# Decode attention on one core: V29 loaded in front of K31, five projections moved behind V29's products, the last projection's weights in three parts

## The chip, the cores and the metric

The kernel runs on one core of one Trainium2 chip. A core has a matrix engine (PE, TensorE), a vector engine (DVE, VectorE), a scalar engine (ACT), GpSimd (POOL) and a queue processor (SP) that here issues nearly all transfers; sixteen DMA engines carry them. The metric is the device time of one execution in microseconds. The kernel before takes 526.45 us (median of 3 runs, 526.36 to 526.49).

## What is computed

One decode step: layer norm of x (4 rows of 640), attention of 32 heads over the last W = 2048 positions of a cache of 8192, a gated feed-forward block, and the sum of both with x. All arrays are bf16.

```python
W = min(4096, max(256, Sk // 4))                      # 2048
q = (xn @ wq).reshape(B, 1, 32, 192).transpose(0, 2, 1, 3)
k = k_cache[:, :, Sk - W:, :]                         # 4 x 32 x 2048 x 192
v = v_cache[:, :, Sk - W:, :]
scores = einsum("bhqd,bhkd->bhqk", q, k) * 192 ** -0.5
o = einsum("bhqk,bhkd->bhqd", softmax(scores), v)
A = o.transpose(0, 2, 1, 3).reshape(B, 1, 32 * 192) @ wo
h = silu(xn @ w1) * (xn @ w3)
out = x + A + h @ w2
```

The K and V windows are 3 MB for each head and kind, 64 such tiles in all; wo is 6144 x 640.

## The kernel before

**Tiles.** A K or V tile holds one head for all 4 batch rows: partition p belongs to batch p // 32, and holds 64 positions of 192 numbers. There are two K buffers (kt) and two V buffers (vt), used in turn by even and odd heads. "K31" is the K tile of head 31, the last one, and so on.

**One head.** VectorE multiplies the K tile by the query in two halves (`mult`, line 271). PE adds the products up over groups of 32 numbers by products with the identity (`adder`, lines 419 and 370), once for each half; VectorE reduces the rest to 64 scores per partition (`reduce_half`, line 277) and takes the maximum over them (`chain_lmax`, 282). PE transposes that column (`tr`, 428), VectorE takes the maximum per batch row (`chain_gmax`, 286), ScalarE scales it (348), PE broadcasts it back over the partitions (`bc`, 432), ScalarE copies it (350) and takes the exponential (352). VectorE spreads the result into z (`chain_z`, 291); PE multiplies z with the V tile in 32 products (`pv`, 445), ScalarE copies the result (355), and PE sums the partial rows (`osum`, 453). For each pair of heads PE makes the softmax sums (`tot`, 437), and VectorE normalizes (`norm_rec`, `norm_og`, 295 and 300); for every fourth head it transposes into oT (303).

**Projections.** `proj(hg)` multiplies the heads of group hg (four heads) with their 768 rows of wo: 6 rows per partition, two products for each, so 12 products of 128x4 by 128x320 (line 382), added into the accumulator acc, in which x and the feed-forward block are already. wo 0 to 4 lie in the buffers wts, loaded during the heads 4 to 8; wo 5, 6 and 7 go into the first K buffer, free once head 30's tile has been multiplied.

**PE's order.** PE runs a hand-written order. A loop takes the heads up to 29 through their adders and up to 28 through their products with V. The end is written out (from line 488): adder 0 of head 30, tr, osum and bc of the heads before, adder 1, tot, proj(0), the products of V29, then the same for head 31 with the products of V30; proj(1), tr of head 31, proj(2), bc, osum of head 30, proj(3), proj(4), tot, the products of V31 in two halves, osum of head 31, and proj(5) to proj(7).

**SP's order.** SP issues transfers in order, and waits in front of each until its buffer is free: `load_k(h)` (line 160) for `s_red` of head h - 2 (its first reduce), `load_v(h)` (168) for `s_pv` of head h - 2 (its products). In the loop of line 181 K(h+2) is followed by V(h+1), up to V28. After the loop come V29, V30 and the two halves of V31, then wo 5, 6 and 7 (lines 197 to 200). So the last tiles come in the order K30, K31, V29, V30, V31. wo 7 comes as five rows and one row, each with a semaphore of its own; PE waits for the first in front of ten products and for the second in front of the last two.

Of the kernel before, what the change touches and what calls it, by code (L numbers as in the profile page):

```python
# [16 lines left out]
def kernel(  # L17
# [15 lines left out]
    B, Sq, D = A_x.shape  # L33
    _, H, Sk, Dh = A_k_cache.shape
# [16 lines left out]
    RPP = QW // P  # L51
# [68 lines left out]
    def sem(name):  # L120
        return ctx.enter_context(nc.semaphore(name))

    first = sem("s_first")
    (s_x, s_wq0, s_wq1, s_wq2, s_w1, s_w3, s_w2, s_k0, s_k1, s_v31, s_wom, s_wo5, s_wo6, s_wo7a, s_wo7b,
     s_gp, s_dv, s_ac, s_pp, s_ps, s_red, s_tr, s_gmax, s_bc, s_negm, s_exp, s_pv, s_sum, s_rec, s_og, s_oT,
     s_tot, s_acc, s_fin, s_done) = [sem(n) for n in (
        "s_x", "s_wq0", "s_wq1", "s_wq2", "s_w1", "s_w3", "s_w2", "s_k0", "s_k1", "s_v31", "s_wom", "s_wo5",
        "s_wo6", "s_wo7a", "s_wo7b", "s_gp", "s_dv", "s_ac", "s_pp", "s_ps", "s_red", "s_tr", "s_gmax", "s_bc",
        "s_negm", "s_exp", "s_pv", "s_sum", "s_rec", "s_og", "s_oT", "s_tot", "s_acc", "s_fin", "s_done")]
    last = sem("s_last")  # L130
    s_pr, s_lmax, s_gneg, s_z, s_v0, s_v1, s_osb, s_out = [sem(n) for n in (
# [4 lines left out]
    def take(e, s, n=1):  # L136
        e.wait_ge(s, n).then_inc(s, -n)  # L137

    def flat(t):
        return (t if isinstance(t, bass.AP) else t[:]).rearrange("p a b -> p (a b)")  # L140
# [5 lines left out]
    def wo_of(hg):  # L146
        t = wts[hg // 2][:, :] if hg < 5 else wo_end
        i = hg % 2 if hg < 5 else hg - 5
        return t[:, i * RPP * D:(i + 1) * RPP * D]

    def wo_src(hg):
        return A_wo[hg * QW:(hg + 1) * QW, :].rearrange("(p i) n -> p (i n)", i=RPP)


    sp = nc.sync

    def load_k(h):
        if h >= 2:
            sp.wait_ge(s_red, 2 * (h - 2) + 1)
        sp.dma_start(out=flat(kt[h % 2]), in_=k_win[:, h].rearrange("b (p j) d -> p b (j d)", p=PB)).then_inc(s_k[h % 2], 16)  # L160

    def load_v(h, j0=0, j1=NJ, s=None):
        if j0 == 0:
            if h >= 2:
                sp.wait_ge(s_pv, h - 1)
            else:
                sp.wait_ge(s_pp, 13)
        sp.dma_start(out=vt[h % 2][:, j0:j1, :].rearrange("q j d -> q (j d)"),
                     in_=v_win[:, h].rearrange("b (p j) d -> p b j d", p=PB)[:, :, j0:j1, :].rearrange("p b j d -> p b (j d)")
                     ).then_inc(s or s_v[h % 2], 16)  # L170
# [9 lines left out]
    load_v(0)  # L180
    for h in range(H - 2):
        load_k(h + 2)
        if h < H - 4:
            load_v(h + 1)
        if h in (4, 6, 8):
            g = h - 4
            n = 2 if g < 4 else 1
            sp.wait_ge(s_pp, 16)
            sp.dma_start(out=wts[g // 2][:, 0:n * RPP * D].rearrange("p (g i) -> p g i", g=n),
                         in_=A_wo[g * QW:(g + n) * QW, :].rearrange("(g p i) n -> p g (i n)", g=n, i=RPP)).then_inc(s_wom, 16)  # L190
    load_v(H - 3)
    load_v(H - 2)
    load_v(H - 1, 0, NJ // 2)
    load_v(H - 1, NJ // 2, NJ, s_v31)
    sp.wait_ge(s_red, 2 * (H - 2) + 1)
    for hg, s in ((5, s_wo5), (6, s_wo6)):
        sp.dma_start(out=wo_of(hg), in_=wo_src(hg)).then_inc(s, 16)
    WC = RPP - 1
    sp.dma_start(out=wo_of(7)[:, 0:WC * D], in_=wo_src(7)[:, 0:WC * D]).then_inc(s_wo7a, 16)
    sp.dma_start(out=wo_of(7)[:, WC * D:], in_=wo_src(7)[:, WC * D:]).then_inc(s_wo7b, 16)  # L200


    gp = nc.gpsimd
# [163 lines left out]
    pe = nc.tensor  # L367

    def held(o, lhsT, rhs, start, stop):
        return pe.add_instruction(mybir.InstMatmult(  # L370
            name=nc.get_next_instruction_name(), engine=pe.engine,
            ins=[pe.lower_ap(rhs), pe.lower_ap(lhsT, for_matmul_weights=True)], outs=[pe.lower_ap(o)],
            start_tensor_calc=start, stop_tensor_calc=stop, ldweights=False))

    pe.wait_ge(s_dv, n_xn)
    for kc in range(KC):
        m = pe.transpose(out=xnT_ps[:, kc, :], in_=xn[:, kc:D:KC], identity=idb[0:B, 0:B])
    m.then_inc(s_pp, 1)

    def acc_add(lhsT, rhs, start=False, stop=False):  # L380
        for i in range(2):
            m = pe.matmul(acc[i * CT:i * CT + B, 0:N0], lhsT=lhsT, rhs=rhs[:, i * N0:(i + 1) * N0], start=start, stop=stop)  # L382
        return m
# [4 lines left out]
    for c0 in (0, 6):  # L388
# [3 lines left out]
        for kc in range(KC):  # L392
# [4 lines left out]
            for i, qp in enumerate(q_banks):  # L397
                m = held(qp, w, wq_rows[kc][:, (c0 + i) * QC:(c0 + i + 1) * QC], kc == 0, kc == KC - 1)
# [3 lines left out]
    for t, bank, s in ((wts[0], po, s_w1), (wts[1], mt, s_w3)):  # L402
# [3 lines left out]
        for kc in range(KC):  # L406
            for w in range(HG):
                m = pe.matmul(bank[w * CT:(w + 1) * CT, 0:FW], lhsT=xnT[:, kc].rearrange("p a b -> p (a b)")[:, 0:CT],
                              rhs=t[:, kc * F + w * FW:kc * F + (w + 1) * FW], start=(kc == 0), stop=(kc == KC - 1))
# [3 lines left out]
    for c in range(FC):  # L413
        m = acc_add(hT[:, c, 0:B], wts[2][:, c * D:(c + 1) * D])
    m.then_inc(s_pp, 1)

    def adder(a):
        take(pe, s_pr)
        pe.ldweights(idb[:])  # L419
        for q in range(2):  # L420
            for kk in range(NK):
                m = held(ps[:, a, q].rearrange("p (j d) -> p j d", d=DD), idb[:], prs[:, a, q, :, kk * DD:(kk + 1) * DD],
                         kk == 0, kk == NK - 1)
        m.then_inc(s_ps, 1)

    def tr(par):
        take(pe, s_lmax)
        pe.transpose(out=mt[0:1, 0:P], in_=lmax[par][:], identity=idf[:]).then_inc(s_tr, 1)  # L428

    def bc(par):  # L430
        take(pe, s_gneg)
        pe.matmul(mt[:, P:P + 1], lhsT=flat(gneg[par]), rhs=one[:], start=True,  # L432
                  stop=True).then_inc(s_bc, 1)

    def tot():
        for par in range(2):
            m = pe.matmul(mt[:, P + 1:P + 2], lhsT=flat(tot_w[:, par]), rhs=rsum[par][:], start=(par == 0), stop=(par == 1))  # L437
        return m

    def pv(par, j0=0, j1=NJ):  # L440
        if j0 == 0:
            take(pe, s_v[par], 16)
        for jj in range(j0 // 2, j1 // 2):
            c = jj % 4
            m = pe.matmul(o_ps[c * CT:c * CT + 2 * B, 0:2 * Dh].rearrange("p (a d) -> p a d", a=2), lhsT=z[par][:, 2 * jj:2 * jj + 2, :],  # L445
                          rhs=vt[par][:, 2 * jj:2 * jj + 2, :], start=(jj < 4), stop=(jj >= NJ // 2 - 4))
        if j1 == NJ:
            m.then_inc(s_pv, 1)

    def osum(par):  # L450
        take(pe, s_osb)
        for k in range(2):
            m = pe.matmul(po[:, 0:Dh], lhsT=flat(sel_w[:, par, k]),  # L453
                          rhs=o_sb[par][:, k * Dh:(k + 1) * Dh].rearrange("p (r i) -> p i r", i=RPP), start=(par + k == 0), stop=(par + k == 2))
        m.then_inc(s_sum, 1)

    def proj(hg, i0=0, i1=RPP):
        w = wo_of(hg)
        for i in range(i0, i1):
            m = acc_add(oT[:, hg, i, 0:B], w[:, i * D:(i + 1) * D], stop=(hg == NG - 1 and i == RPP - 1))  # L460
        return m
# [30 lines left out]
    adder(1)  # L492
    take(pe, s_z)
    tot()
    pe.wait_ge(s_wom, 48)
    pe.wait_ge(s_oT, 5)
    proj(0)
    pv(1)
    adder(0)
    tr(0)  # L500
    osum(1)
# [1 line left out]
    adder(1)  # L503
    take(pe, s_z)
    pv(0)
    proj(1)
    tr(1)
    proj(2)
    bc(1)
    osum(0)  # L510
    proj(3)
    proj(4)
    take(pe, s_z)
    tot().then_inc(s_tot, 1)
    pv(1, 0, NJ // 2)
# [6 lines left out]
    pe.wait_ge(s_wo6, 16)  # L522
    proj(6)
    pe.wait_ge(s_oT, 8)
    pe.wait_ge(s_wo7a, 16)
    proj(7, 0, WC)
    pe.wait_ge(s_wo7b, 16)
    proj(7, WC, RPP).then_inc(s_acc, 1)
    work.close()


# [33 lines left out]
```

## Time and profile before

| what | value |
|---|---|
| median of 3 runs | 526.45 us (526.36 to 526.49) |
| the profiled execution, its own time | 526.31 us |
| its span, first to last instruction | 524.5 us |
| mean granted TensorE clock | 0.86 |
| HBM read | 222.96 MB, 425 GB/s over the span |
| PE busy | 364.7 us (70%) |
| VectorE busy | 334.1 us (64%) |
| ScalarE busy | 54.5 us (10%) |
| last instruction of PE ends | 521.63 us |

An engine's share is busy time over the span. The profile's DMA line gives, for 40 equal slices of the span, the mean busy share of the sixteen DMA engines in tenths; a queue's line gives packets, MB and the share of the engines' time. A group's line has the line of the kernel, the engine, the operation, the tile written and those read, the shapes and the number of instructions; then busy us, the mean ns of one, and the idle time in front of them with what ended it. In the timeline each line is a start, a duration (both us, from the first instruction) and a group of like instructions that follow each other; in brackets the idle time before it. Matmuls are pipelined, so a group's duration is the time from its first start to its last end.

### The profile page before, as it was taken

How to read it: one execution, taken by the hardware profiler on the slowest of the kernel's cores; microseconds unless marked ns; L12 is line 12 of the kernel's file. 1: busy time of each engine (PE TensorE's matmuls, PEld its weight loads, DVE VectorE, ACT ScalarE, POOL GpSimd, SP SyncE). 2: the span in 40 equal slices, each digit the busy share in tenths (PEclk: the TensorE clock that was granted, in tenths of full speed). 3: DMA queues.
4: the chain of work that ended last, by engine and by line, in shares of the span. 5: the costliest groups of instructions: out<-in, count | busy, mean ns of one | idle time of the engine just before them, and what ended most of it. 6: DMA issues, size and time to landing. Idle time of an engine off the chain costs nothing. (4 is left out here: it accounts for less than half of the span.)

```text
span 524.5 us, 4777 instructions
## 1 busy us (share of the span) xinstructions
PE 364.7 (70%) x2306; PEld 83.9 (16%) x1553; DVE 334.1 (64%) x286; ACT 54.5 (10%) x175; POOL 3.0 (1%) x16
## 2 busy tenths in 40 slices
PE   2775767676587375876666767687676767687797
PEld 0020101110111011111120112111121112111134
DVE  2136767676367564678776666667776666666871
ACT  2120201010101011011010111110110011111011
POOL 2000000000000000000000000000000000000000
PEclk9887888797878799788797888988788888888799
DMA  8999999999999999999999999999999999999995
GB/s 358 423 439 429 425 437 422 442 427 424 443 427 437 429 428 435 439 427 439 427 439 429 427 439 425 439 429 435 433 427 439 425 440 429 433 435 427 439 419 244
DMA packets 11512, 223.07 MB, mean 425 GB/s; under 512 B 1256, under 2 KB 1392, under 8 KB 2416
## 3 DMA queue, kind: packets, MB, share of 16 engines
q1 hardware_dynamic: 11488, 222.96, 99.0%
q8 instruction: 4, 0.07, 0.0%
q14 instruction: 4, 0.03, 0.0%
q10 hardware_dynamic: 16, 0.01, 0.0%
HBM read 222.96 MB, written 0.01 MB: 425 GB/s over the span
## 5 line engine op out<-in xcount | busy, mean ns | idle before, releaser
L370 PE MATMUL ps<-prs,idb 128*128 128x512 bf16 x768 | 227.7, 459 | 134.6 <-PEq L137 134.6
L271 DVE TENSOR_TENSOR prs<-kt,qbc 128x6144 bf16<-128x6144 bf16 x64 | 214.5, 3353 | 117.6 <-DMA kt<-in_A_k_cache_dram 117.6
L277 DVE TENSOR_REDUCE sc<-ps 128x32 f32<-128x1024 f32 x64 | 77.5, 1211 | 3.1 <-PE ps L370 2.9
L453 PE MATMUL po<-o_sb,sel_w 128*128 128x192 f32 x128 | 49.0, 516 | 0.7 <-PEq L137 0.7
L445 PE MATMUL o_ps<-vt,z 128*8 128x384 bf16 x1024 | 47.2, 326 | 0.1
L348 ACT ACTIVATE gneg<-gmax 1x128 f32<-1x128 f32 x32 | 9.8, 308 | 290.1 <-DVE gmax L286 290.1
L445 PEld LDWEIGHTS o_ps<-vt,z 128*8 128x8 bf16 x1024 | 22.1, 86 | 54.7 <-issue 42.1
L419 PEld LDWEIGHTS <-idb 128*128 128x128 bf16 x64 | 6.3, 98 | 153.3 <-issue 152.8
L453 PEld LDWEIGHTS po<-o_sb,sel_w 128*128 128x128 f32 x128 | 25.6, 223 | 14.3 <-issue 4.9
L355 ACT COPY o_sb<-o_ps 128x384 f32<-128x384 f32 x32 | 15.3, 478 | 117.5 <-PE o_ps L445 117.5
L291 DVE TENSOR_TENSOR z<-ex,mask_b 128x256 bf16<-128x256 bf16 x32 | 13.5, 422 | 19.6 <-ACT ex L352 19.2
L428 PEld LDWEIGHTS mt<-idf,lmax 128*1 128x1 f32 x32 | 3.3, 103 | 117.9 <-issue 117.9
L286 DVE TENSOR_REDUCE gmax<-mt 1x4 f32<-1x128 f32 x32 | 8.9, 277 | 12.7 <-PE mt L428 12.3
L432 PE MATMUL mt<-one,gneg 1*128 1x1 f32 x64 | 11.9, 253 | 4.9 <-PEq L137 4.8
L231 DVE CAST qbc<-ps 128x512 bf16<-128x512 f32 x4 | 2.6, 686 | 20.0 <-PE ps L370 20.0
L437 PEld LDWEIGHTS mt<-rsum,tot_w 128*128 128x128 f32 x64 | 9.6, 191 | 35.1 <-issue 34.7
L370 PE MATMUL ps<-vt,xnT 128*128 128x512 bf16 x31 | 10.7, 480 | 5.5 <-DMA vt<-in_A_wq_dram 4.4
L432 PEld LDWEIGHTS mt<-one,gneg 1*128 1x128 f32 x64 | 9.4, 182 | 23.4 <-issue 23.4
L352 ACT ACTIVATE ex<-sc,negm 128x64 bf16<-128x64 f32 x32 | 11.1, 348 | 1.0
L428 PE MATMUL mt<-idf,lmax 128*1 128x128 f32 x32 | 10.5, 327 | 0.0
L300 DVE TENSOR_SCALAR og<-po,rt 64x192 bf16<-64x192 f32 x16 | 6.6, 413 | 3.8 <-PE po L453 3.6
L350 ACT COPY negm<-mt 128x1 f32<-128x1 f32 x32 | 5.1, 159 | 29.2 <-PE mt L432 29.2
(65 smaller groups left out, 81.9 us busy)
## 6 DMA issues: line engine op xcount, KB each, us to landing
kt<-in_A_k_cache_dram SPq DMA_DIRECT2D x32, 3072.0 KB, 19.6
vt<-in_A_v_cache_dram SPq DMA_DIRECT2D x31, 3072.0 KB, 22.6
vt<-in_A_wq_dram SPq DMA_DIRECT2D x2, 3072.0 KB, 13.2
wt<-in_B_w_dram SPq DMA_DIRECT2D x3, 1920.0 KB, 27.8
wt<-in_A_wo_dram SPq DMA_DIRECT2D x2, 1920.0 KB, 27.8
vt<-in_A_v_cache_dram SPq DMA_DIRECT2D x2, 1536.0 KB, 10.8
kt<-in_A_wo_dram SPq DMA_DIRECT2D x2, 960.0 KB, 14.6
prs<-in_A_wq_dram SPq DMA_DIRECT2D x1, 1536.0 KB, 19.8
```

Source lines behind the costliest of these rows:

```text
L271: ve.tensor_tensor(out=prs[:, a].rearrange("p q j d -> p (q j) d"), in0=kt[h % 2][:, 2 * a * JQ:2 * (a + 1) * JQ, :], in1=qbc[:, h * Dh:(h ...
L277: ve.tensor_reduce(out=sc[h % 3][:, 2 * a * JQ:2 * (a + 1) * JQ], in_=ps[:, a].rearrange("p q (j d) -> p (q j) d", d=DD), axis=AX.X, op=AL ...
L291: ve.tensor_tensor(out=z[h % 2][:], in0=ex[h % 2][:].unsqueeze(2).to_broadcast([P, NJ, B]), in1=mask_b[:].unsqueeze(1).to_broadcast([P, NJ ...
L348: ae.mul(out=gneg[h % 2][:], in_=gmax[h % 2][:].unsqueeze(1).to_broadcast([1, PB, B]), mul=-SCALE).then_inc(s_gneg, 1)
L352: ae.activation(out=ex[h % 2][:], in_=sc[h % 3][:], func=ACTF.Exp, bias=negm[h % 2][:, 0:1], scale=SCALE, accum_out=rsum[h % 2][:]).then_i ...
L355: ae.copy(out=o_sb[h % 2][:], in_=o_ps[:, 0:2 * Dh]).then_inc(s_osb, 1)
L370: return pe.add_instruction(mybir.InstMatmult(name=nc.get_next_instruction_name(), engine=pe.engine, ins=[pe.lower_ap(rhs), pe.lower_ap(lh ...
L428: pe.transpose(out=mt[0:1, 0:P], in_=lmax[par][:], identity=idf[:]).then_inc(s_tr, 1)
L432: pe.matmul(mt[:, P:P + 1], lhsT=flat(gneg[par]), rhs=one[:], start=True, stop=True).then_inc(s_bc, 1)
L437: m = pe.matmul(mt[:, P + 1:P + 2], lhsT=flat(tot_w[:, par]), rhs=rsum[par][:], start=(par == 0), stop=(par == 1))
L445: m = pe.matmul(o_ps[c * CT:c * CT + 2 * B, 0:2 * Dh].rearrange("p (a d) -> p a d", a=2), lhsT=z[par][:, 2 * jj:2 * jj + 2, :], rhs=vt[par ...
L453: m = pe.matmul(po[:, 0:Dh], lhsT=flat(sel_w[:, par, k]), rhs=o_sb[par][:, k * Dh:(k + 1) * Dh].rearrange("p (r i) -> p i r", i=RPP), star ...
```

## The change

V29 is issued inside the loop, behind K30 and in front of K31, as the loop does for the V tiles before. The order of the last tiles becomes K30, V29, K31, V30, V31. In PE's order proj(0) leaves its place in front of V29's products, and proj(1) to proj(4) leave their places in head 31's round; all five follow V29's products. wo 7 comes in three parts of three, two and one rows, each with a semaphore, and PE waits for each in front of its products.

```diff
     for h in range(H - 2):
         load_k(h + 2)
-        if h < H - 4:
+        if h < H - 3:
             load_v(h + 1)
...
-    load_v(H - 3)
     load_v(H - 2)
     load_v(H - 1, 0, NJ // 2)
     load_v(H - 1, NJ // 2, NJ, s_v31)
...
-    WC = RPP - 1
-    sp.dma_start(out=wo_of(7)[:, 0:WC * D], in_=wo_src(7)[:, 0:WC * D]).then_inc(s_wo7a, 16)
-    sp.dma_start(out=wo_of(7)[:, WC * D:], in_=wo_src(7)[:, WC * D:]).then_inc(s_wo7b, 16)
+    last_cols = ((0, 3, s_wo7a), (3, 5, s_wo7b), (5, RPP, s_wo7c))
+    for i0, i1, s in last_cols:
+        sp.dma_start(out=wo_of(7)[:, i0 * D:i1 * D], in_=wo_src(7)[:, i0 * D:i1 * D]).then_inc(s, 16)
...
     tot()
+    pv(1)
     pe.wait_ge(s_wom, 48)
     pe.wait_ge(s_oT, 5)
-    proj(0)
-    pv(1)
+    for g in range(5):
+        proj(g)
     adder(0)
     tr(0)
     osum(1)
...
     pv(0)
-    proj(1)
     tr(1)
-    proj(2)
     bc(1)
     osum(0)
-    proj(3)
-    proj(4)
     take(pe, s_z)
     tot().then_inc(s_tot, 1)
     pv(1, 0, NJ // 2)
...
     pe.wait_ge(s_oT, 8)
-    pe.wait_ge(s_wo7a, 16)
-    proj(7, 0, WC)
-    pe.wait_ge(s_wo7b, 16)
-    proj(7, WC, RPP).then_inc(s_acc, 1)
+    for i0, i1, s in last_cols:
+        pe.wait_ge(s, 16)
+        m = proj(7, i0, i1)
+    m.then_inc(s_acc, 1)
```

The list of semaphores gains `s_wo7c`.

## The prediction

> **What bounds the kernel now.** I read the page first: slices, queues, groups.
>
> ```profile
> DMA  8999999999999999999999999999999999999995
> q1 hardware_dynamic: 11488, 222.96, 99.0%
> L271 DVE TENSOR_TENSOR prs<-kt,qbc 128x6144 bf16<-128x6144 bf16 x64 | 214.5, 3353 | 117.6 <-DMA kt<-in_A_k_cache_dram 117.6
> ```
>
> The transfers take 99.0% of the sixteen engines' time, and no slice but the first and the last is below 9: up to the tail the kernel is a stream of 223 MB, and VectorE waits 117.6 us for K tiles. The change moves no byte, so the stream cannot end sooner by it. What can move is the order of the last tiles and the computing behind them. The chain that ended last, in order of time, shows what ends now:
>
> ```profile
> 517.49 1.58 PE po L453 x4
> 519.07 2.56 PE acc L382 x36
> ```
>
> These are osum of head 31 and the projections 5 to 7. They run without a gap, though the two parts of wo 7 landed only at 503.3 + 16.9 = 520.2 and 504.7 + 15.9 = 520.6 us (issue times and times to landing of lines 199 and 200). If PE were early, the two products of wo 7's last row would still wait for 520.6. I then took the timeline of the tail. Columns are start, us, engine, line, operation.
>
> ```profile
> 484.55 3.36 DVE L271 TENSOR_TENSOR prs<-kt,qbc 128x6144 bf16<-128x6144 bf16 x1 [4.05 <-DMA kt<-in_A_k_cache_dram]
> 496.19 3.35 DVE L271 TENSOR_TENSOR prs<-kt,qbc 128x6144 bf16<-128x6144 bf16 x1
> 499.19 1.47 PE L445 MATMUL o_ps<-vt,z 128*8 128x384 bf16 x32
> 500.60 2.76 PE L370 MATMUL ps<-prs,idb 128*128 128x512 bf16 x12
> 500.92 3.35 DVE L271 TENSOR_TENSOR prs<-kt,qbc 128x6144 bf16<-128x6144 bf16 x1
> 505.22 2.76 PE L370 MATMUL ps<-prs,idb 128*128 128x512 bf16 x12
> 509.28 0.22 DVE L282 TENSOR_REDUCE lmax<-sc 128x1 f32<-128x64 f32 x1
> 510.13 0.27 PE L428 MATMUL mt<-idf,lmax 128*1 128x128 f32 x1
> 511.24 0.38 PE L432 MATMUL mt<-one,gneg 1*128 1x1 f32 x2
> 511.55 1.61 PE L453 MATMUL po<-o_sb,sel_w 128*128 128x192 f32 x4
> 512.32 0.43 DVE L291 TENSOR_TENSOR z<-ex,mask_b 128x256 bf16<-128x256 bf16 x1 [1.60 <-ACT ex L352]
> 513.08 1.79 PE L382 MATMUL acc<-wt,oT 128*4 128x320 bf16 x24
> 515.34 1.47 PE L445 MATMUL o_ps<-vt,z 128*8 128x384 bf16 x32
> ```
>
> The multiply at 484.55 (head 30) waits for K30, that at 496.19 (head 31) for nothing: K31, issued at 479.4, took 12.4 us and landed at 491.8. V29, issued at 479.95, took 19.1 and landed at 499.05, so the products of V29 at 499.19 are what waits. z of head 31 is ready at 512.75 (512.32 + 0.43), but PE is in projections 3 and 4 until 514.81, and V31's products start only at 515.34. So the tail has two costs today: V29's landing, and projections that stand in PE's order in front of V31's products.
>
> **V29 in front of K31.** SP issues in order. load_v(29) waits for the products of V27, done at 468.14 + 1.47 = 469.61; load_k(31) for head 29's first reduce, done at 479.3. V29 goes out near 469.7, K31 at 479.4 as now; one instruction each, no more DMAs. Nothing is held behind the new place: V30 behind them still waits for 483.5 (V28's products). The queue is full (K30 lands at 484.5), and the two tiles are equally large (3072 KB), so they swap landings: V29 at 491.8, K31 at 499.05. The cadence of K tiles says the same: the waiting multiplies start at 455.46, 469.99, 484.55, which gives 499.1. So head 31's multiply starts at **499.1 instead of 496.19, 2.9 us later**. VectorE's sequence is fixed from there: in head 29 the second multiply starts 4.67 us after the first (469.99 to 474.66), here at 503.77, and ends at 507.12 (now 500.92 + 3.35 = 504.27).
>
> **Projections 0 to 4 behind V29's products.** V29 is there, so its products start 3.03 us after the adder at 495.08, as in head 29's round (465.11 to 468.14): 498.11, without projection 0 (0.98 us) in front. The 60 projection products come 1.30 us later (V30's products at 507.92, the next projection at 509.22): 499.41. Twelve took 0.91 us to PE's next operation (510.33 to 511.24), twenty-four 1.73 (513.08 to 514.81): 0.068 each beyond the start, so sixty take 1.73 + 36 x 0.068 = 4.2 us, and head 31's first adder starts at **503.6, now 500.60**. The multiply it needs ends at 502.5, so 3.1 us of the projections lie in a hole, 1.1 us stick out. Behind that adder stand tr, osum and bc, and then the second adder, now 4.62 us later (505.22): 508.22. VectorE's own path comes out alike: multiply end 507.12, max 0.03 on, gneg 0.31 on, its end 0.31 on, bc 0.14 on (504.80 to 504.94), adder 0.28 on: 508.2. So the second adder is **3.0 us late**, whichever leads. Bounds of the sixty: 5 x 0.98 = 4.9 (504.3, so 0.7 more), and at the low end no more than the hole, which gains nothing, since VectorE's path stands.
>
> **What the projections leave behind.** Head 31's score maximum starts at 509.28 + 3.0 = 512.28 and ends at 512.50. Its transpose stood behind projection 1 (lmax ended at 509.50, tr began at 510.13); now it needs a semaphore's time, 0.11 (a multiply's end at 487.91 to its weight load at 488.02): 512.61. So 0.5 us is given back; bounds 0.1 and the 0.63 of now. From tr to bc 1.11 as now: 513.72. From bc to the end of z 1.51 (511.24 to 512.75): 515.23. osum starts 0.31 behind bc and holds PE for 1.53 (511.55 to 513.08): 514.03 to 515.56, a little later than z. There tot follows at once, not behind 1.73 us of projections 3 and 4, and 0.53 later V31's products: **516.09 instead of 515.34**. If PE needs a fresh start at tot (0.58 us is the idle row of its weight loads beside osum), 516.7.
>
> **Wo 7 in three parts.** One more DMA and two waits moved. The issues lie near 505, ten us before the data, and the last landing stays 520.6. From V31's products to the end of PE 6.29 us pass (515.34 to 521.63), so the end falls at 522.4, with every landing past: the split is worth nothing here, and would be worth up to 0.7 us if PE came early. If the third part cost one more issue of the longest kind (1.27 us), the landing would be at 521.9, and the last of the three parts is not needed before 522.2.
>
> **Sum.** +3.0 (second adder of head 31) - 0.5 (tr no longer behind projection 1) - 1.75 (V31's products no longer behind projections 3 and 4) = **+0.75 us**. The profiled run took 526.31 (span 524.5 and 1.8 around it), so it would be 527.06; the median 526.45 lies 0.14 above that run, so I say **527.2**. What a measurement tells apart is about 0.2%, 1.05 us: the forecast is no change, on its slow side. Its own range is +0.4 (0.35 of lags saved) to +1.05.
>
> **Rivals.** *The projections hold PE longer (slower).* From an adder start of 503.6 on, each further microsecond is one of the total, since VectorE's path no longer hides it. With the 0.98 us row five times, 504.3 and +1.45; with the late start at tot besides, +2.0: **527.9 to 528.5**. For it: the rows of 12 and 24 are short, and sixty in a row are not in this trace. Against it: the same step of 0.068 in both.
>
> *The clock falls (slower).* Four windows of the granted clock (the share behind POOL):
>
> ```profile
> 452.40:455.70 3.30, 2.19 (x36) 0.69 (x32) 0.24 (x1) 0.48 (x1) 0.00 (x0) 1.00 1.04 447
> 483.10:486.40 3.30, 0.35 (x12) 0.00 (x0) 1.85 (x1) 0.48 (x1) 0.00 (x0) 1.00 1.04 447
> 486.50:493.20 6.70, 5.15 (x13) 0.30 (x3) 6.12 (x4) 0.00 (x0) 0.00 (x0) 0.50 0.97 418
> 513.70:517.10 3.40, 3.12 (x54) 1.75 (x50) 0.17 (x1) 0.23 (x1) 0.00 (x0) 1.00 1.02 422
> ```
>
> PE was busy 0.35 us in the window at 483.1, and the next 6.7 us ran at 0.50. A window with 2.19 busy (452.4) did not do that. If narrow products counted as idle, the stretch from 500 to 503.5, now all projections, would halve the clock at head 31's adder: head 30, at 0.50, needed 7.03 us from adder to adder (488.05 to 495.08) and not 4.62, so 2.4 us more: **529.6**. Against it: 513.7 to 517.1 held only tot, projections and V's products, and the clock stayed at 1.00. [...]
>
> *The end goes to the landing of wo 7 (faster).* If PE had V31's products by 514.7, the end would be 520.6 plus one row of wo 7 and its drain, 0.4 us: 521.0, so **525.8**. For it: 1.75 us of projections leave the end. Against it: head 31's second multiply cannot end before 507.1 behind a K31 of 499.05. To be faster by over 0.2% the stream would have to end 0.4 us sooner as well.
>
> *The swap doesn't happen*: V29 waits behind something that the trace does not show, and K31 stands behind it. Nothing speaks for it; at K31's present landing, 525.8 too, later without a bound.
>
> **How the numbers follow.** Forecast 52%, of which 4 reach above 527.5; longer hold of PE 26%; clock 8%; landing of wo 7 10%, of which 5 below 525.4; no swap 4%, one of them faster. Faster 0.06, within 0.2% 0.56, slower 0.38. The range, 526.0 to 528.5, takes in the forecast and the long hold; it leaves out the fallen clock and the landing case.
>
> **What would show it.** After: head 31's first multiply at 499.1 with a K tile as releaser; V29's products at 498.1; sixty products in a row to 503.5; second adder near 508.2; tr 0.1 behind lmax; V31's products at 516.1; last landing 520.6 and no wait for it. The forecast is wrong if head 31's multiply starts before 498, if the clock after 500 is below 1.00, or if V31's products start before 515.3 or after 517.

## The result and the profile after

| | before | after |
|---|---|---|
| median | 526.44 us (526.29 to 527.35, 17 runs) | 528.3 us (526.67 to 529.59, 17 runs) |
| ratio after to before, 95% interval | | 1.0025 (1.0016 to 1.0035) |
| profiled execution, its span | 526.31, 524.5 us | 528.81, 526.3 us |
| last instruction of PE ends | 521.63 us | 523.44 us |

The change is slower by 0.25%. The median lies 1.1 us above the forecast of 527.2 and inside the range that was given, 526.0 to 528.5. The median stands for few runs, though: the 17 fall into **two groups**, seven at 526.67 to 527.00 and ten at 528.12 to 529.59, with nothing between. Before had no such split. The page of the changed kernel, its DMA slices, the load queue and the K multiply:

```profile
DMA  8999999999999999999999999999999999999994
q1 hardware_dynamic: 11632, 222.96, 98.7%
L270 DVE TENSOR_TENSOR prs<-kt,qbc 128x6144 bf16<-128x6144 bf16 x64 | 214.5, 3353 | 121.3 <-DMA kt<-in_A_k_cache_dram 121.3
```

The stream is as full as before, up to the last slice, and VectorE waits 3.7 us more for K tiles (121.3 against 117.6): that is head 31's wait of 4.03 us for K31 in the timeline below, which before's timeline does not have, less small gains at other heads. The chain that ended last is the same two pieces, 1.81 us later:

```profile
519.30 1.58 PE po L452 x4
520.88 2.56 PE acc L381 x36
```

The tail in the timeline of the changed kernel (start us, us, engine, line, operation):

```profile
496.97 1.47 PE L444 MATMUL o_ps<-vt,z 128*8 128x384 bf16 x32
498.27 4.24 PE L381 MATMUL acc<-wt,oT 128*4 128x320 bf16 x60
499.16 3.36 DVE L270 TENSOR_TENSOR prs<-kt,qbc 128x6144 bf16<-128x6144 bf16 x1 [4.03 <-DMA kt<-in_A_k_cache_dram]
502.67 2.75 PE L369 MATMUL ps<-prs,idb 128*128 128x512 bf16 x12 [0.16 <-PEq L137]
508.13 2.76 PE L369 MATMUL ps<-prs,idb 128*128 128x512 bf16 x12
512.18 0.22 DVE L281 TENSOR_REDUCE lmax<-sc 128x1 f32<-128x64 f32 x1
512.55 0.27 PE L427 MATMUL mt<-idf,lmax 128*1 128x128 f32 x1 [0.26 <-PEq L137]
513.62 0.35 PE L431 MATMUL mt<-one,gneg 1*128 1x1 f32 x2 [0.80 <-PEq L137]
514.67 0.42 DVE L290 TENSOR_TENSOR z<-ex,mask_b 128x256 bf16<-128x256 bf16 x1 [1.54 <-ACT ex L351]
515.33 0.90 PE L436 MATMUL mt<-rsum,tot_w 128*128 128x1 f32 x4
516.16 2.46 PE L444 MATMUL o_ps<-vt,z 128*8 128x384 bf16 x32
```

Head 31's multiply now waits for a K tile and starts at 499.16 (forecast 499.1). The sixty products fill PE's wait for it. The second adder starts at 508.13 (508.2), tr at 512.55 (512.6), tot at 515.33 (515.56). These four agree with the prediction within 0.25 us; V29's products and head 31's first adder came about 1 us earlier than forecast, which the second adder does not show. Then V31's products take 2.46 us, not the 1.47 of those of the other heads. The windows of that stretch follow. Each line has the window, its length, the busy us of PE, its weight loads, VectorE, ScalarE and GpSimd (instructions in brackets), the granted clock, the DMA share and GB/s:

```profile
511.40:514.80 3.40, 2.34 (x30) 1.32 (x21) 1.38 (x4) 1.39 (x5) 0.00 (x0) 1.00 0.98 405
514.80:518.20 3.40, 3.40 (x35) 1.94 (x37) 0.47 (x2) 0.00 (x0) 0.00 (x0) 0.50 0.99 411
```

The clock is at 0.50 for 3.4 us, just under tot and V31's products. My theory from here (A): the upper group is this fall; it happens because projections 1 to 4 no longer fill the gaps of head 31's softmax chain; the lower group is the change without it. Rivals: the groups come from the transfers, or from what lies around the span.

### The profile page after: what moved, and what is told of

The parts are those of the page before. It is cut to its first block, busy times and chain, and to the rows that moved or that the text cites. A ratio compares the mean times of both kernels' runs of the same rounds, so it can differ in the third digit from the quotient of the medians.

```text
span 526.3 us, 4778 instructions
## 1 busy us (share of the span) xinstructions
PE 365.7 (69%) x2306; PEld 84.7 (16%) x1553; DVE 334.3 (64%) x286; ACT 54.5 (10%) x175; POOL 3.0 (1%) x16
## 5 line engine op out<-in xcount | busy, mean ns | idle before, releaser
L270 DVE TENSOR_TENSOR prs<-kt,qbc 128x6144 bf16<-128x6144 bf16 x64 | 214.5, 3353 | 121.3 <-DMA kt<-in_A_k_cache_dram 121.3
L444 PEld LDWEIGHTS o_ps<-vt,z 128*8 128x8 bf16 x1024 | 22.3, 87 | 56.3 <-issue 44.0
L436 PE MATMUL mt<-rsum,tot_w 128*128 128x1 f32 x64 | 8.4, 235 | 0.0
## 6 DMA issues: line engine op xcount, KB each, us to landing
kt<-in_A_k_cache_dram SPq DMA_DIRECT2D x32, 3072.0 KB, 19.6
```

What stands on the lines that cost most here:

```text
L270: ve.tensor_tensor(out=prs[:, a].rearrange("p q j d -> p (q j) d"), in0=kt[h % 2][:, 2 * a * JQ:2 * (a + 1) * JQ, :], in1=qbc[:, h * Dh:(h ...
```

## The experiments

**The changed kernel once more, unaltered.**

> The changed kernel once more, unaltered, for a second profile. Theory A: if this profiled run is of the lower group (526.6 to 527.1), the clock is 1.00 through V31's products, which take 1.47 us and not 2.46, and they start near 516.0; if of the upper (528.1 to 529.6), it shows the fall to 0.50 between 511 and 519 again. Rival (the groups come from elsewhere): an upper run with the clock at 1.00 throughout, or a lower one with the fall.

Median 526.95 us of 10 runs, again two groups: seven at 526.74 to 527.15, three at 529.21 to 529.57. The profiled run took 526.84, so it is of the lower group; its timeline and one window:

```profile
508.22 2.76 PE L369 MATMUL ps<-prs,idb 128*128 128x512 bf16 x12
512.64 0.27 PE L427 MATMUL mt<-idf,lmax 128*1 128x128 f32 x1 [0.26 <-PEq L137]
515.43 0.52 PE L436 MATMUL mt<-rsum,tot_w 128*128 128x1 f32 x4
515.88 1.47 PE L444 MATMUL o_ps<-vt,z 128*8 128x384 bf16 x32
```

```profile
510.80:514.20 3.40, 2.34 (x37) 1.27 (x37) 1.72 (x3) 0.89 (x3) 0.00 (x0) 1.00 0.98 411
```

From the second adder to tot the two profiles of one kernel agree within 0.1 us, although the sixty products (499.57) and head 31's first adder (503.75) start 1.3 and 1.1 us later in this one. Here tot and V31's products run at full clock (1.00 from 514.20 to 517.60), and PE ends at 522.16 instead of 523.44; osum of head 31 starts at 518.03 instead of 519.30. Of these 1.27 us, tot to V31's products makes 0.38 (0.83 against 0.45) and from there to osum 0.99 (3.14 against 2.15), less 0.10 of a later start. The two runs differ by 1.97 us, though: the spans (526.3 and 525.0) by 1.3, and the other 0.67 lies around the span, where this fall does not explain it.

In both traces the clock changes only at edges that are 3.41 us or a multiple of it apart (in the first profile the last four changes are at 487.49, 490.90, 514.80 and 518.21 us; before's trace has the same step, with changes at 476.23, 486.47 and 493.29). With this step the edges in the tail are 511.38, 514.80 and 518.21 us in the first profile and 510.83 and 514.24 in the second, so the windows lie 0.6 us differently over the same work. PE's busy share alone doesn't decide: it is 2.34 of 3.4 us in both. The first window holds 0.91 us of V30's products beside tr, bc and osum, the second 1.55 us of the adder and V30's products.

**Filler in the gap.** If the fall comes from PE's gaps, any work there must end it.

```diff
     tr(1)
+    pe.ldweights(idb[:])
+    for i in range(4):
+        held(ps[:, 0, i % 2].rearrange("p (j d) -> p j d", d=DD), idb[:], prs[:, 0, i % 2, :, 0:DD], True, True)
     bc(1)
     osum(0)
```

> The changed kernel with four products of 128x128 by 128x512 more on PE between tr and bc of head 31; they write scores' sums that nobody reads any more, and they take 4 x 0.216 = 0.86 us of a gap that is 1.1 us long. Theory A (the two groups of the changed kernel's runs, 526.7 to 527.0 and 528.1 to 529.6, are the granted clock, which falls to 0.50 behind a window in which PE waits for head 31's softmax chain): no run above 527.3, median 526.8 us, and the clock is 1.00 from 491 to the end of PE. Rival 1 (the two groups come from the transfers or from the start and end of the execution): still both groups and a median near 528.3 us. Rival 2 (the filler makes bc late): 527.1 to 527.5 in the faster group and the slower group still there.

Median 526.97 us, all eleven runs at 526.72 to 527.12; ratio to before 1.0003 (0.9994 to 1.0012). The timeline shows the filler and V31's products, the window the same stretch as in the first profile (this run's own edges are 510.05, 513.46 and 516.88; between the first two PE is busy 3.15 of 3.41 us):

```profile
512.78 1.02 PE L369 MATMUL ps<-prs,idb 128*128 128x512 bf16 x4
513.74 0.37 PE L431 MATMUL mt<-one,gneg 1*128 1x1 f32 x2
515.92 1.47 PE L444 MATMUL o_ps<-vt,z 128*8 128x384 bf16 x32
```

```profile
511.40:514.80 3.40, 3.14 (x38) 1.32 (x24) 1.37 (x3) 1.39 (x5) 0.00 (x0) 1.00 0.99 412
```

Of the unaltered kernel's 27 runs 13 are in the upper group, with 0.86 us of work that computes nothing none of 11. That speaks against the rival causes, since the filler touches neither transfers nor the ends of the execution. Only one run of the upper group has a trace, so that the clock fell in this place in all 13 is inferred from the filler and not seen.

**A projection as the filler.**

```diff
-    for g in range(5):
+    for g in range(4):
         proj(g)
...
     tr(1)
+    proj(4)
     bc(1)
```

> The changed kernel with projection 4 put between tr and bc of head 31 (0.8 us of work in a gap of 1.1), and projections 0 to 3 behind V29's products. Theory A (work in that gap keeps the clock, whatever work it is): one group, median 526.8 us, no run above 527.5, V31's products at 516.0 and 1.47 us long. [...]

Median 527.08 us; ten runs at 526.75 to 527.22 and one at 529.21; ratio 1.0013 (1.0004 to 1.0022). So ten of eleven runs stay in the lower group with narrow products in the gap; had those counted as idle, the split of 13 in 27 would have been expected again. In the profiled run, one of the ten (527.03), the clock is at 1.00 from 509.7 to 516.5, and V31's products start at 516.07 and take 1.47 us. Whether the one run is a window that the products did not fill is not shown, as it has no trace. With work of either kind in the gap 1 run of 22 is in the upper group, without it 13 of 27.

**The load order alone** (V29 in front of K31; the rest as before).

> Only V29 is loaded in front of K31; projections and wo 7 stay as before. Theory A (K31's late landing costs 3.0 us at head 31's second adder, and nothing is given back as long as projections 1 to 4 stay in head 31's round): head 31's first multiply starts at 499.1 with a K tile as releaser, its first adder near 502.6, its second adder near 508.2 (before: 505.22), V31's products near 518.3 (before: 515.34), the median 526.45 + 3.0 = 529.4 us, with little spread, since PE has projections in its gaps. Rival (VectorE's lateness is hidden, since V29's products no longer wait for their tile): the second adder stays at 505 to 506 and the median at 526.4 to 527.

Median 530.52 us (530.03 to 531.21, 5 runs); ratio 1.0069 (1.0056 to 1.0082). Slower than either theory said. Its timeline and windows:

```profile
499.51 3.36 DVE L270 TENSOR_TENSOR prs<-kt,qbc 128x6144 bf16<-128x6144 bf16 x1 [4.24 <-DMA kt<-in_A_k_cache_dram]
503.01 4.44 PE L369 MATMUL ps<-prs,idb 128*128 128x512 bf16 x12 [3.63 <-PEq L137]
509.15 2.77 PE L369 MATMUL ps<-prs,idb 128*128 128x512 bf16 x12
519.27 1.47 PE L444 MATMUL o_ps<-vt,z 128*8 128x384 bf16 x32
```

```profile
500.10:503.50 3.40, 0.48 (x3) 0.10 (x1) 3.40 (x2) 0.00 (x0) 0.00 (x0) 1.00 0.97 412
503.50:506.90 3.40, 3.40 (x10) 0.00 (x0) 3.40 (x4) 0.00 (x0) 0.00 (x0) 0.50 0.97 411
```

K31's lateness is there, and nothing of it is given back. On top PE idles 3.63 us, the clock falls, and the first adder takes 4.44 us. I had left that out: in this kernel no projections fill the wait. A third part is neither: 2.2 to 2.9 us lie around the span in all five runs, against 1.8 to 1.9 in the runs of before beside them.

**The load order alone, with filler in that wait.**

```diff
     proj(0)
     pv(1)
+    pe.ldweights(idb[:])
+    for i in range(12):
+        held(ps[:, 0, i % 2], idb[:], qbc[:, 0:QC], True, True)
```

> V29 in front of K31 alone, with twelve filler products of 128x128 by 128x512 (2.6 us) behind V29's products, in PE's wait for K31; their sums nobody reads. Theory A (of the 4.05 us that the load order alone cost, 3.0 are K31's late landing and about 1 the clock that fell in the unfilled wait): head 31's first adder takes 2.76 us, its second adder starts at 508.2, the median is 529.4 us. Rival (all 4 us are the landing's): 530.5 as without filler; or (all is the clock's): 526.5 to 527.

Median 529.69 us: four runs at 529.38 to 529.73, two at 531.45 and 532.34, which have no trace.

```profile
499.67 3.36 DVE L270 TENSOR_TENSOR prs<-kt,qbc 128x6144 bf16<-128x6144 bf16 x1 [3.34 <-DMA kt<-in_A_k_cache_dram]
503.18 2.75 PE L369 MATMUL ps<-prs,idb 128*128 128x512 bf16 x12
508.64 2.76 PE L369 MATMUL ps<-prs,idb 128*128 128x512 bf16 x12
```

From the multiply to the second adder 8.97 us pass here and 9.64 without filler: 0.67 us is the clock's part, and 8.97 is also the way in the changed kernel (499.16 to 508.13). So about 3 us of the order's cost is the landing: 529.69 against 526.63 before, with 529.4 forecast (K31's multiply itself came 0.5 us later in this run than in the changed kernel's).

**The projections alone** (0 to 4 behind V29's products; V29 still lands behind K31).

> Only projections 0 to 4 are moved behind V29's products; V29 still lands at 499.05 behind K31, and wo 7 stays in two parts. Theory A: V29's products start at 499.2, the sixty products of the projections hold PE from 500.5 to 504.6, head 31's first adder starts at 504.7 (before: 500.60) and its second adder at 509.3; then 2.25 us come back (0.5 at tr, 1.75 at V31's products): V31's products at 517.2, 526.45 + 4.1 - 2.25 = 528.3 us; where the clock falls as in the changed kernel, up to 2 us more. Rival (the projections out of the tail are worth their 1.75 us without the new load order, as they fill idle time): 525.8 us, the landing of wo 7.

Median 528.23 us of 7 runs, ratio 1.0036 (1.0021 to 1.0052): four at 527.78 to 528.23, three at 529.70 to 530.47. The profiled run is of the upper three:

```profile
500.86 4.24 PE L382 MATMUL acc<-wt,oT 128*4 128x320 bf16 x60
505.04 2.77 PE L370 MATMUL ps<-prs,idb 128*128 128x512 bf16 x12
509.51 2.76 PE L370 MATMUL ps<-prs,idb 128*128 128x512 bf16 x12
517.54 2.45 PE L445 MATMUL o_ps<-vt,z 128*8 128x384 bf16 x32
```

Without the new order the sixty products are on the path: VectorE has head 31's first half done at 499.0, and its adder waits for PE until 505.04. The clock falls under V31's products here too (0.50 from 516.2 to 519.5), so this fall belongs to the projections' move and not to the order.

**Wo 7 in three parts alone.**

> Only wo 7 comes in three parts of three, two and one rows; order of V29 and K31 and the projections stay as before. Theory A: the parts land near 519.3, 520.1 and 520.6 us, PE still ends near 521.6, and the median is 526.4 us (within 0.2). Rival (smaller transfers cost the stream time, or a third DMA its issue): the last landing is 521.9 and the median 527.3 us or more.

Median 526.99 us, before on the same chip 526.67; ratio 1.0003 (0.9994 to 1.0012): no difference clear of the scatter. The median lies 0.6 us above the forecast of 526.4, and seven of the eleven runs have 0.3 to 0.6 us more around the span than before. PE ended at 521.76 in the profiled run, as forecast.

**The projections at the end of the loop, new load order.** V28's products leave PE idle for K30; the projections can go there.

```diff
         pe.reg_add(cnt, cnt, 1)
+    pe.wait_ge(s_wom, 48)
+    pe.wait_ge(s_oT, 5)
+    for g in range(5):
+        proj(g)
     adder(0)
...
     pv(1)
-    pe.wait_ge(s_wom, 48)
-    pe.wait_ge(s_oT, 5)
-    for g in range(5):
-        proj(g)
     adder(0)
```

> The changed kernel with projections 0 to 4 moved to the end of the loop, so that nothing fills PE's wait for K31 behind V29's products. Theory A (K31's late landing sets the end whatever the projections do, and an unfilled wait costs the clock): V29's products end near 498.4, PE idles 4 us, the clock falls to 0.50 by about 503.5 in most runs, head 31's first adder takes 4 to 5 us and not 2.76, and the median is 527.8 to 529.5 us. Rival (the sixty products held PE, and the time of the changed kernel is theirs): 526.0 to 526.8.

Median 528.91 us of 12 runs; nine at 528.64 to 529.85, three at 526.82 to 526.91. The profiled run, of the nine:

```profile
502.83 5.28 PE L369 MATMUL ps<-prs,idb 128*128 128x512 bf16 x12 [4.43 <-PEq L137]
509.90 2.76 PE L369 MATMUL ps<-prs,idb 128*128 128x512 bf16 x12
517.56 1.47 PE L444 MATMUL o_ps<-vt,z 128*8 128x384 bf16 x32
```

PE idles 4.43 us for K31 and the first adder takes 5.28 us. The three lower runs, which have no trace, are as fast as the changed kernel's lower group. So the sixty products in the wait cost nothing there, and K31's landing is enough to set that time.

**The projections at the end of the loop, old load order, wo 7 in three parts.**

> The load order of before (K31 in front of V29), wo 7 in three parts, and projections 0 to 4 moved to the end of the loop, behind V28's products, where PE idles from 483.5 to 488.0 us for K30. Theory A (before, PE's tail was late by the projections in head 31's round alone, and the stream's last landing is the floor): the sixty products run from 483.5 to 487.7, head 30's first adder starts at 488.0 as before, now at the full clock; head 31's second adder stays at 505.2, V31's products start near 513.1 (before: 515.34), and PE ends 0.4 us behind the last landing of 520.6: 525.8 us. If the clock falls in head 31's chain too, PE still has 2 us of slack. Rival (the sixty products are late for head 30's first adder, or the fallen clock reaches the end): 526.5 to 528.

Median 526.56 us, ratio 0.9997 (0.9988 to 1.0006): five runs at 525.73 to 526.14, six at 526.56 to 527.13. The profiled run took 525.85:

```profile
483.82 4.24 PE L382 MATMUL acc<-wt,oT 128*4 128x320 bf16 x60
488.25 2.75 PE L370 MATMUL ps<-prs,idb 128*128 128x512 bf16 x12 [0.18 <-PEq L137]
513.45 2.45 PE L445 MATMUL o_ps<-vt,z 128*8 128x384 bf16 x32
518.09 3.07 PE L382 MATMUL acc<-kt,oT 128*4 128x320 bf16 x36
```

The sixty products fit the wait for K30, V31's products start 1.9 us earlier than before, and even with the clock at 0.50 PE catches up with the stream: its weight loads wait 0.46 and 0.32 us for the last parts of wo 7. PE ends at 521.16, 0.31 us behind the start of the last weight loads at 520.85; the 0.4 us of the forecasts were an estimate. So this run, one of the five, ends at the floor that the last landing sets; the six do not reach it, and their times are the rival's. The trace also shows that products 4 columns wide held the clock: between the edges 484.76 and 488.18 PE has nothing but projections (busy 3.30 us), and the clock stays at 1.00; head 30's first adder behind them takes 2.75 us, where before, behind 4.60 us without work, it took 5.28.

**The same with filler,** four products between tr and bc of head 31 and two behind V31's products.

> The kernel with projections 0 to 4 at the end of the loop and the old load order, with filler on PE whose sums nobody reads: four products of 128x128 by 128x512 between tr and bc of head 31, two behind V31's products. Theory A (the upper half of that kernel's runs, 526.6 to 527.1, is again the fallen clock in head 31's chain): one group at 525.7 to 526.1, median 525.8 us, V31's products 1.47 us long. Rival (the upper half comes from the stream, whose last landing varies): both halves again, median 526.4 to 526.6.

Median 526.87 us of 12 runs, ratio 1.0007 (0.9998 to 1.0015): three runs at 525.80 to 526.09, nine at 526.65 to 528.68. The theory missed: the split stays. In the profiled run, of the three, V31's products take 1.63 us, with a wait of 0.38 for V31's second half, and PE waits for wo:

```profile
518.73 0.98 PE L382 MATMUL acc<-kt,oT 128*4 128x320 bf16 x12 [0.62 <-DMA kt<-in_A_wo_dram]
519.99 1.40 PE L382 MATMUL acc<-kt,oT 128*4 128x320 bf16 x12 [0.28 <-DMA kt<-in_A_wo_dram]
```

So in that run the end belongs to the stream and what follows it. What makes the upper part of these two kernels is open; no trace of such a run was taken. No version tried beats both kernels clear of the scatter.

## Why the prediction was right, and where it fell short

**The number: in the range in part by luck.** The range went up to 528.5 for a longer hold of PE by the projections, which did not occur. The fallen clock, which did, the prediction left out of its range and named as a sign of being wrong. That 528.3 lies in the range follows from ten upper runs among the first 17: over all 27 runs of the kernel, 14 of them lower, the median is 527.15 us, and it stands for neither group's middle. The steps behind the number are told one by one below.

**V29 in front of K31, +3.0 us at the second adder: right.** 508.13 and 508.22 in two profiles, against 505.22 before: 2.9 to 3.0. The tiles swapped their landings as forecast: V29 landed at 491.9 (issued at 469.6, 22.3 us to landing), K31 at 499.2 (479.6 and 19.6). The order alone with the wait filled cost 3.0 us in the median (529.69 against 526.63). Two readings of the prediction are off and change no forecast: the rows at 465.11 and 468.14 belong to head 28's round, not head 29's, and before's maximum at 504.18 starts 0.09 us ahead of the multiply's end, not 0.03 behind.

**The sixty products, 4.2 us, 3.1 of them in the wait: right.** They take 4.24 us from first start to last end in both profiles. In the second profile V29's products start at 498.27 (forecast 498.11), the sixty at 499.57 (499.41) and head 31's first adder at 503.75 (503.6), so 1.2 us of them stick out behind the multiply. In the first profile V29's products start at 496.97: there head 30's first adder took 4.11 us, in the second profile and before 5.28. So the adder behind the sixty starts at 502.67, when the multiply is done, and nothing sticks out. The second adder comes within 0.1 us at the same time in both: VectorE's path sets it, as the prediction's low bound had it. The rival in which they hold PE longer did not occur. With the old order they take 4.24 us as well, but there they are on the path, and the projections alone cost 1.6 us.

**tr 0.5 us given back: right.** 512.55 is 2.42 later than before, with an adder 2.91 later: 0.49.

**V31's products no longer behind projections 3 and 4, -1.75 us: right in half of the runs.** In the lower group they start at 515.88, 0.54 later than before, and PE ends 0.53 later (522.16 against 521.63; forecast 0.75); the time is 526.84 against 526.31, and the group's median, 526.82, is 0.38 above before's. In the upper group this term failed. Projections 1 to 4 were a cost in head 31's round, and also work in the window that kept PE's clock through its softmax chain (before, PE is busy 3.40 of 3.40 us from 510.30 to 513.70, and the clock is at 1.00 up to the end of PE's work). The 1.75 us counted the cost alone. In the traced upper run, without them, PE has gaps of 0.26 and 0.80 us (before tr and before bc) in one window, the clock falls, and 1.27 us are lost under tot and V31's products. In the two traces it is how the windows happen to lie over this work that decides; for the untraced runs that is likely and not shown. The spans of the thirteen upper runs are 526.2 to 527.7 us, 1.2 to 2.7 above the 525.0 of the traced lower run, so some of them lost more than this fall, and where is not shown.

**The clock rival: the clock fell, but for another reason, at another place and more often.** The rival got 8%; it had narrow products count as idle and the clock fall at 503.5, behind the projections, for 529.6 us. Narrow products did not count as idle: with nothing but projections between 484.76 and 488.18 (busy 3.30 us, above) the clock stayed at 1.00. The traced fall came at 514.8, behind the stretch that the projections had left, and 13 of 27 runs are in the group that it stands for. I had argued that a window with 2.19 us busy did no harm, from one window at 452.4. Its work was another: the end of an adder and all of V's 32 products, where here a part of V30's products, tr, bc and a part of osum stand. Two windows with 2.34 busy, one with the fall and one without, show that this row could not carry the argument. Two more traces have the fall at this place, the projections alone and at the end of the loop with the old order: their windows (512.73 to 516.14 and 508.66 to 512.07) hold 0.94 and 0.91 us of products with V, against 0.91 in the changed kernel's. What exactly the clock counts as busy the runs do not show. In the changed kernel's window (511.38 to 514.80) no gap was longer than 0.80 us: two short gaps in one window, 1.06 us together, were enough in that run.

**Wo 7 in three parts: nothing, right.** PE waited for the last landing only in the two kernels with the projections at the end of the loop and the old load order, whose V31's products started at 513.45 and 513.32.

**The parts together.** Alone they cost 3.9, 1.6 and, within the scatter, 0 us (530.52, 528.23 and a ratio of 1.0003, against 526.67). Together the order takes V29's wait away from the projections and the projections fill the wait for K31, which leaves 0.4 us in the lower group and 2.4 in the upper (median of its ten 528.85).

## What to carry to other kernels

Before work is moved off PE, look at what stays behind in each window between two edges of the clock (here 3.41 us), not only at the longest gap: here a window with 2.34 us busy and gaps of 0.26 and 0.80 us was followed by 3.41 us at 0.50. Movable work was worth most in a wait that would otherwise be empty (the order alone, with the wait for K31 unfilled, cost 3.9 us, the changed kernel's lower group 0.4), and a piece of it belonged in the gaps of the last dependent chain (with projection 4 there 1 of 11 runs is in the upper group, with nothing there 13 of 27). In a full queue the tile whose reader has the longest chain behind it goes first: here the swap put the 3072 KB of V29 in front of K31, which landed 7.4 us later, and head 31's second adder started 3.0 us later. Where the runs of a kernel split into groups, one profile tells one group's story; take another before explaining the median.

## What the runs showed that was not expected

- The clock fell behind a window in which PE was busy 2.34 of 3.4 us with no gap over 0.80 us, and with the same share it did not fall in another run of the same kernel.
- What lies around the span is not constant. It is 1.8 to 2.0 us in all runs of before that have a span on record, and 2.5 to 3.1 us in five of the first ten upper runs of the changed kernel (528.81 with a span of 526.3 is one). With wo 7 in three parts alone it is 2.2 to 2.4 us in seven of eleven runs, which have spans of 524.6 to 524.8. It makes up to 1.2 us of the upper group. The five profiled runs in which it is 2.2 us or more have an instruction fetch of 8 to 24 KB that starts 1.8 to 2.1 us behind the last instruction; of the seven with 1.8 to 1.9 us six have none, and one has it 0.7 us behind. What brings the fetch about was not tried and stays open.
- With the same load order, head 31's multiply started at 499.16, 499.33, 499.51 and 499.67 us in the profiles of four kernels: the landing of K31 scatters by half a microsecond between them.
